# First stage of an attention and feed-forward kernel: the reciprocal's first value in the unit's own PSUM bank, other result latencies for the planner, another order

## The chip, the cores and the metric

The kernel runs on one core of one Trainium2 chip. The metric is the device time of one execution in microseconds (us), the median of several runs. A core has TensorE (PE), which multiplies matrices and writes only PSUM; VectorE (DVE) and ScalarE (ACT), which read and write PSUM and SBUF; GpSimd (POOL), which here works on SBUF only; and SyncE (SP), whose queue issues all DMAs of this kernel. Each engine carries out its instructions in the order of the program. In the profile "PEld" is the loading of a matmul's stationary operand, which overlaps the matmuls.

## The reference

Block-causal attention over 8 batches, 8 heads, 576 positions of width 64 (blocks of 64 positions), and after it a feed-forward layer of 4608 tokens, 512 to 2048 to 512, whose activation is a rational function:

```python
scores = scale * np.matmul(q, k.transpose(0, 1, 3, 2))
scores = np.where(mask, scores, -1000000000.0)      # mask: block_i >= block_j
scores = scores - np.max(scores, axis=-1, keepdims=True)
attn = np.exp(scores)
attn = attn / (np.sum(attn, axis=-1, keepdims=True) + 1e-09)
x = np.matmul(attn, v)                              # then heads side by side: 4608 x 512
h = x @ w_in
h2 = h * h
h3 = h2 * h
P = a[0] + a[1] * h + a[2] * h2 + a[3] * h3
Q = 1.0 + np.abs(b[0]) * np.abs(h) + np.abs(b[1]) * h2
g = P / (Q + 1e-6)
out = g @ w_out
```

All tensors are float32.

## The kernel before

**Precision.** Matmuls run on rounded float32 (fp32r). Each operand is split into a high and a low part, and a product is three matmuls: high by low, high by high, low by high.

**Planner.** Nothing is issued while the kernel is described. Every piece of work becomes an `op` of the class `Plan`: an engine, a planned cost, a priority (`pri`, lower goes first), the buffers it reads and writes, and a function that emits the instructions. `Plan.order` then simulates the engines with the planned costs, takes at each step the operation that can start first (by priority among those that are ready), and the instructions are emitted in that one order, so each engine's queue is fixed by it. `LATENCY` (L66) is the time that the planner adds between the end of an operation and the start of one on another engine that needs it, by the engine that consumes. `PORT` (L65) is added to the planned cost of an operation marked `port=True`, which is used for DVE operations with two operands in SBUF. `gate` holds back an operation until attention has come to within 12 priority units of it.

**Banks.** PSUM's eight banks form one pool, `banks`. A `Buf` takes a slot when its first operation is planned and gives it back after its last. Quotas limit how many banks one use may hold: six for attention (`QA`), two for the first product of a feed-forward unit in the first stage (`QH`), two for its output accumulators (`QO`). The third argument of `Buf` (`keep`) is the number of slots that must stay free when it takes its own.

**Attention.** The eight heads of a batch are taken in pairs, 32 pairs in all, and pair `p` has priorities around `10 * p`. `load` (L380) issues six DMAs for q, k and v; from the third pair on, q and k share one raw buffer. `prep` (L400) transposes q or k on PE (L409) and splits it into high and low on ACT and DVE (L413, L416); for these pairs DMAs copy the parts into the operand tiles `kq`. `vprep` (L441) splits v on ACT and POOL. `scores` (L465) takes five query tiles: score matmuls (L508, L509), maximum on DVE (L520), exponential with sum on ACT (L524), reciprocal of the sum (L531 to L536), normalization on POOL (L538, L544), transposes of the probabilities on PE (L565) and their split on ACT and DVE (L580, L582). `pv` (L589) multiplies with v and writes the result to DRAM scratch (L603 to L621).

**Feed-forward.** The first half of the hidden width is done for 15 chunks of 256 tokens beside attention (`ffn0`, L708, "first stage"), four units per chunk, so 60 units; a unit is 256 hidden values: the first product into one bank `h` (L740), the rational function on 128 x 512 values (`wide`, L675), and the second product (L759). Weights are split by `place` (L625), which `split_weights` (L656) calls: 16 blocks that stay on the chip and 16 that go to DRAM scratch, with priorities spread over a span of attention's. The rest of the feed-forward is done after attention (`ffn1`, L822, "second stage"), whose `wide` calls have `rpsum` set: its reciprocal has a PSUM bank of its own.

**`wide`.** The denominator is built in SBUF tiles: |h| in `ut` (L677), then POOL (L680, L682). The numerator is built in `st` from `h` (L678, L684, L686). The reciprocal of the denominator starts as the exponential of minus its logarithm (L688, L692), is improved by a Newton step (L694, L696) and multiplied with the numerator (L698). ACT and POOL split the result into `gh` and `gl` (L701, L702). In the first stage the reciprocal's first value goes into `vt`, an SBUF tile, so that L694, L696 and L698 have two operands in SBUF.

Of the kernel before, what the change touches and what calls it, by code (L numbers as in the profile page):

```python
# [14 lines left out]
ALU = mybir.AluOpType  # L15
# [13 lines left out]
NFA = 8  # L29
NFB = NF - NFA  # L30
# [4 lines left out]
QC = 1.0 + 1e-6  # L35
# [27 lines left out]


PORT = 220.0  # L65
LATENCY = {"PE": 90.0, "ACT": 40.0, "DVE": 40.0, "POOL": 90.0, "SP": 60.0, "-": 0.0}  # L66


class Plan:
# [161 lines left out]
def attn_ffn_kernel(  # L231
# [22 lines left out]
    banks = Pool([ps.tile([128, 512], F32, name=f"ps{chr(97 + i)}") for i in range(8)])  # L254

    QA, QH, QO, QH1, QO1, QR1, QR = (Pool([None] * n) for n in (6, 2, 2, 2, 4, 2, 1))

    def tiles(pool_, n, shape, dt, name):
# [4 lines left out]
    wscr = ([dpool.tile([128, 4, NFB * 128], F32, name=f"wscri{x}") for x in "hl"]  # L263
            + [dpool.tile([128, NFB, DM], F32, name=f"wscro{x}") for x in "hl"])
# [16 lines left out]
    a0, a1 = coef[:, 0:1], coef[:, 1:2]  # L281
# [9 lines left out]
    QR = tiles(att, 1, [LP, 2 * NL, D], F32, "qr")  # L291
# [88 lines left out]
    def load(p):  # L380
        b, hp = divmod(p, NPAIR)
        h0 = 2 * hp
        pri = 10 * p - 12 + 3
        s = {}
        for which, src in ((0, q), (1, k)):
            r = s["raw", which] = Buf(OS if which and p < NATP else QR)
            for j in range(2):
                aop("SP", sp(147, True), lambda r=r, j=j, src=src: nc.sync.dma_start(
                    out=rows(r)[:, j::2, :], in_=src[b, h0 + j].rearrange("(c p) d -> p c d", p=LP)),
                    wr=[(r, j)], pri=pri + 2 * which)  # L390
        vr = s["vr"] = Buf(VR)
        for j in range(2):
            aop("SP", sp(16, True, 2), lambda j=j: nc.sync.dma_start(
                out=vr.t[j * 64:(j + 1) * 64, 0, :], in_=v[b, h0 + j, 0:64, :]), wr=[(vr, j, 0)], pri=pri + 5)
            aop("SP", sp(131, True), lambda j=j: nc.sync.dma_start(
                out=vr.t[:, 1 + j::2, :], in_=v[b, h0 + j, 64:S, :].rearrange("(c p) d -> p c d", p=128)),
                wr=[(vr, j, 1)], pri=pri + 5)
        return s

    def prep(p, s, which):  # L400
        pri = 10 * p - 10 + (3, 5)[which]
        raw, sc = s["raw", which], (QSCALE, 1.0)[which]
        hl = s["hl", which] = Buf((HLE if p < NATP and p % 2 else HL)[which])
        for half in range(2):
            bank = Buf(banks, QA, 1)

            def tp(half=half, bank=bank):
                for c in range(3):
                    nc.tensor.transpose(bank.t[:, c * LP:(c + 1) * LP], rows(raw)[:, 2 * (half * 3 + c):2 * (half * 3 + c) + 2].rearrange("p j d -> p (j d)"), ident[:LP, :LP])  # L409

            cs = slice(half * 288, half * 288 + 288)
            aop("PE", tr(3, LP), tp, rd=[(raw, 0), (raw, 1), "ident", (hl, "claim")], wr=[bank], pri=pri)
            aop("ACT", act(288), lambda bank=bank, cs=cs: nc.scalar.activation(  # L413
                out=hl.t[:, 0, cs], in_=bank.t[:, :288], func=AF.Copy, scale=sc),
                rd=[bank], wr=[(hl, 0, half)], pri=pri)
            aop("DVE", dve(288), lambda bank=bank, cs=cs: nc.vector.scalar_tensor_tensor(  # L416
                out=hl.t[:, 1, cs], in0=bank.t[:, :288], scalar=sc, in1=hl.t[:, 0, cs].bitcast(F32),
                op0=ALU.mult, op1=ALU.subtract), rd=[bank, (hl, 0, half)], wr=[(hl, 1, half)], pri=pri)
        if p < NATP:
            return  # L420
        H_, L_ = [(hl, 0, 0), (hl, 0, 1)], [(hl, 1, 0), (hl, 1, 1)]
        for j in range(2):
            kq = kqt[p % 2][j]
            own = kq[64 * j:64 * j + 64].bitcast(F32)
            other = kq[64 - 64 * j:128 - 64 * j].bitcast(F32)

            def src(j=j):
                return hl.t[64 * j:64 * j + 64].bitcast(F32)

            def dma(o_, i_, rd, key, kb=147, dims=2):  # L430
                aop("SP", sp(kb * 1.6, dims=3), lambda: nc.sync.dma_start(out=o_, in_=i_()), rd=rd,
                    wr=[("kq", p % 2, j, key)], pri=pri + 0.2 * j)

            if which == 0:
                dma(own[:, 0:2], lambda src=src: src()[:, 0].unsqueeze(1).to_broadcast([64, 2, S]), H_, "q0", 294)
                dma(other[:, 1], lambda src=src: src()[:, 1], L_, "q2")
            else:
                dma(own[:, 2:4], lambda src=src: src(), H_ + L_, "k0", 294)
                dma(other[:, 3], lambda src=src: src()[:, 0], H_, "k1")

    def vprep(p, s):  # L441
        vr = s["vr"]
        pri = 10 * p + 6
        at = [lambda x: x[0:64, 0:64].unsqueeze(1), lambda x: x[64:128, 64:128].unsqueeze(1),
              lambda x: x[:, 128:].rearrange("p (b c) -> p b c", c=192)[:, :, 0:64],
              lambda x: x[:, 128:].rearrange("p (b c) -> p b c", c=192)[:, :, 128:192]]
        of = [lambda: vr.t[0:64, 0:1], lambda: vr.t[64:128, 0:1], lambda: vr.t[:, 1:9:2], lambda: vr.t[:, 2:9:2]]
        keys = [[(vr, 0, 0)], [(vr, 1, 0)], [(vr, 0, 1)], [(vr, 1, 1)]]
        for i, (f, src, rd) in enumerate(zip(at, of, keys)):
            n = 64 if i < 2 else 256  # L450
            vh, vl = (f(x) for x in vpad)
            aop("ACT", (0.833 * n + 110, 0.833 * n + 200), lambda vh=vh, src=src: nc.scalar.copy(out=vh, in_=src()),  # L452
                rd=rd, wr=[("v", i, 0)], pri=pri, after=init_v if p == 0 else ())
            aop("POOL", pool(n, True), lambda vh=vh, vl=vl, src=src: nc.gpsimd.tensor_tensor(  # L454
                out=vl, in0=src(), in1=vh.bitcast(F32), op=ALU.subtract),
                rd=rd + [("v", i, 0)], wr=[("v", i, 1)], pri=pri, after=init_v if p == 0 else ())
# [8 lines left out]
    def scores(p, s, t):  # L465
# [32 lines left out]
        for j in range(2):  # L498
            pri = 10 * p + 2 * t + j
# [47 lines left out]
                    rd=[rc] + [(pt, jj, i) for i in range(np_)], wr=[(pt, "n", jj)], pri=pri)  # L547

        np1 = 128 if t == 0 else nq
        pri += 3  # L550
        nb = 1 + 2 * t
        groups = {1: [1], 3: [1, 2], 5: [1, 4], 7: [4, 3], 9: [3, 3, 3]}[nb]
        blk = 0
        for gi, gn in enumerate(groups):
            bank = Buf(banks, QA, 1)

            def trans(bank=bank, blk=blk, gn=gn):
                for i in range(gn):
# [97 lines left out]
    def split_weights(w, f0, nf, pris, scr):  # L656
        wih, wil, woh, wol = w
        pris = iter(pris)
        for f in range(0, nf, 2):
            cs = slice(f * 128, f * 128 + 256)  # L660
            for d in range(0, 4, 2):
                src = w_in[d * 128:(d + 2) * 128, (f0 + f) * 128:(f0 + f + 2) * 128]
                place(wih[:, d:d + 2, cs], wil[:, d:d + 2, cs], src.rearrange("(d p) f -> p d f", p=128),
                      next(pris), scr, f"wi{f0}_{f}_{d}")
            for d in range(f, f + 2):
                place(woh[:, d:d + 1, :], wol[:, d:d + 1, :],
                      w_out[(f0 + d) * 128:(f0 + d + 1) * 128, :].rearrange("(d p) e -> p d e", p=128),
                      next(pris), scr, f"wo{f0}_{d}")
# [6 lines left out]
    def wide(h, hf, pools, pri, rpsum, xk, tag):  # L675
# [11 lines left out]
            out=st.t, in0=st.t, scalar=a1, in1=h.t, op0=ALU.subtract, op1=ALU.mult), rd=hf, wr=[st], pri=pri)  # L687
        op("ACT", act(512, False, 1), lambda: nc.scalar.activation(out=vt.t, in_=ut.t, func=AF.Ln, bias=qcb),  # L688
           rd=[ut, "qcb"], wr=[vt], pri=pri)
        r0 = Buf(banks, QR1 if rpsum else QR) if rpsum or 0 else vt  # L690
        rq = r0 is vt
        op("ACT", act(512, False), lambda: nc.scalar.activation(out=r0.t, in_=vt.t, func=AF.Exp, scale=-1.0),  # L692
           rd=[] if rq else [vt], wr=[r0], pri=pri)
        op("DVE", dve(512), lambda: nc.vector.scalar_tensor_tensor(  # L694
            out=ut.t, in0=ut.t, scalar=QC, in1=r0.t, op0=ALU.add, op1=ALU.mult), rd=[r0], wr=[ut], pri=pri, port=rq)
        op("DVE", dve(512), lambda: nc.vector.scalar_tensor_tensor(  # L696
            out=r0.t, in0=ut.t, scalar=-2.0, in1=r0.t, op0=ALU.add, op1=ALU.mult), rd=[ut], wr=[r0], pri=pri, port=rq)
        op("DVE", dve(512, 1), lambda: nc.vector.scalar_tensor_tensor(  # L698
            out=st.t, in0=st.t, scalar=a0, in1=r0.t, op0=ALU.subtract, op1=ALU.mult), rd=[r0], wr=[st], pri=pri, port=rq)
        gh, gl = Buf(pools[3]), Buf(pools[4])  # L700
        op("ACT", act(512, False), lambda: nc.scalar.copy(out=gh.t, in_=st.t), rd=[st], wr=[gh], pri=pri)  # L701
        op("POOL", pool(512, True), lambda: nc.gpsimd.tensor_tensor(  # L702
# [81 lines left out]
        pv(p, 0)  # L784
        pv(p, 1)
    op("-", (0, 0), lambda: None, after=early, pri=0, gives=[(X, i) for i in range(3)])
    split_weights(wA, 0, NFA, [0 + 30 * i / NPLA for i in range(NPLA)], False)
    split_weights(wscr, NFA, NFB, [110 + 200 * i / NPLB for i in range(NPLB)], True)
    E0, E1 = 50, 340
    EARLY = ()  # L790
    U0 = [list(range(EARLY[c] if c < len(EARLY) else 4 if c < NCH - 3 else 0)) for c in range(NCH)]
    NU0 = sum(map(len, U0))
# [156 lines left out]
```

## Time and profile before

| | |
|---|---|
| Time, median of 3 runs | 1313.12 us (1309.43 to 1316.41) |
| Profiled execution | 1311.25 us |
| Its span, first to last instruction | 1309.5 us |
| Mean granted clock of TensorE | 0.988 |
| Busy PE / DVE / ACT / POOL | 1245.8 / 972.5 / 893.7 / 898.0 us |
| Busy share PE / DVE / ACT / POOL | 95 / 74 / 68 / 69% |
| Moved by DMA | 195.13 MB, mean 149 GB/s |

A profile is of one execution. In the rows of 40 slices each digit is the busy share of a slice of the span in tenths. Rows of groups end with busy time, mean time of one, idle time of the engine before them and what ended it. Rows of stretches give for each engine the busy time and, in brackets, the number of instructions. Matmuls are pipelined and their ends are modelled, so a PE that reads busy is not always at its peak rate.

### The profile page before, as it was taken

The numbers are of one execution on the slowest core, as the hardware profiler recorded it, in microseconds if no ns is written. First come the engines' busy times: TensorE is split into PE (matmuls) and PEld (weight loads), VectorE is DVE, ScalarE is ACT, GpSimd is POOL, SyncE is SP. The second block draws the span as 40 slices with busy tenths as digits, with TensorE's granted clock in tenths as the row PEclk, the third lists the DMA queues.
The fourth block names the chain that finished last, engine by engine and source line by source line (L and its number), as shares of the span: only waits on it lengthen the run. The fifth ranks groups of instructions, "written<-read, shape, count | busy, mean of one in ns | idle before, by whom it ended". The sixth has DMA issues, their size and how long they took to land.

```text
span 1309.5 us, 23194 instructions
## 1 busy us (share of the span) xinstructions
PE 1245.8 (95%) x7560; PEld 1095.3 (84%) x7560; DVE 972.5 (74%) x1916; ACT 893.7 (68%) x2230; POOL 898.0 (69%) x1218
## 2 busy tenths in 40 slices
PE   7778899999999999999999999999999999999997
PEld 5668799888889888898888889888888888888886
DVE  7877867777778877887887877766666776677665
ACT  5776777777778777787776777655655555555554
POOL 5766876777688867777876777566666666666664
PEclk9888899999999999999999999999999999999999
DMA  5797746777768667768766761750223242324010
GB/s 147 216 240 195 193 126 175 185 181 201 190 169 212 188 178 197 196 190 207 185 181 174 192 179 52 254 189 1 97 88 105 66 129 87 106 66 129 13 53 33
DMA packets 222617, 195.13 MB, mean 149 GB/s; under 512 B 129312, under 2 KB 183584, under 8 KB 222496
## 3 DMA queue, kind: packets, MB, share of 16 engines
q1 hardware_dynamic: 222496, 193.65, 53.8%
q8 instruction: 60, 0.98, 0.3%
q14 instruction: 61, 0.50, 0.1%
HBM read 95.95 MB, written 44.56 MB: 107 GB/s over the span
## 4 chain that ended last, share of the span: by engine, by line
PE 64%; POOL 10%; DMA 8%; DVE 8%; ACT 6%; issue 3%; SPq 1%; POOLq 0%; ACTq 0%; DVEq 0%
PE pse L854 4%; PE psd L854 4%; PE psf L880 4%; PE psg L880 3%; PE psc L880 3%; PE psh L880 2%; PE psb L880 2%; PE psa L880 2%; PE psa L854 2%; PE psb L854 2%; PE psc L759 2%; DMA osa<-in_moe_w_out_dram 2%; PE psh L854 2%; PE psh L740 1%; PE psa L740 1%
## 5 line engine op out<-in xcount | busy, mean ns | idle before, releaser
L680 POOL TENSOR_SCALAR vb<-ua,bab 128x512 f32<-128x512 f32 x58 | 44.8, 772 | 91.1 <-ACT ua L677 90.9
L680 POOL TENSOR_SCALAR va<-ub,bab 128x512 f32<-128x512 f32 x55 | 43.7, 795 | 85.1 <-ACT ub L677 85.0
L454 POOL TENSOR_TENSOR vpl<-vra,vph 128x256 fp32r<-128x256 f32 (+1 forms) x128 | 75.6, 598 | 21.8 <-ACT vph L452 14.5
L702 POOL TENSOR_TENSOR glb<-sa,ghb 128x512 fp32r<-128x512 f32 x60 | 77.7, 1294 | 15.7 <-ACT ghb L701 15.6
L702 POOL TENSOR_TENSOR gla<-sb,gha 128x512 fp32r<-128x512 f32 x57 | 74.1, 1301 | 8.3 <-ACT gha L701 7.7
L682 POOL TENSOR_TENSOR ua<-vb,ua 128x512 f32<-128x512 f32 x58 | 75.9, 1308 | 4.6
L682 POOL TENSOR_TENSOR ub<-va,ub 128x512 f32<-128x512 f32 x55 | 71.3, 1296 | 4.3
L688 ACT ACTIVATE va<-ub,qcb 128x512 f32<-128x512 f32 x55 | 39.8, 724 | 47.9 <-POOL ub L682 47.7
L688 ACT ACTIVATE vb<-ua,qcb 128x512 f32<-128x512 f32 x58 | 42.2, 727 | 41.6 <-POOL ua L682 41.6
L701 ACT CAST ghb<-sa 128x512 fp32r<-128x512 f32 x60 | 37.4, 624 | 22.3 <-DVE sa L698 22.0
L740 PE MATMUL psh<-x,wiha 128*128 128x256 f32 x272 | 51.2, 286 | 0.0
L701 ACT CAST gha<-sb 128x512 fp32r<-128x512 f32 x57 | 35.4, 622 | 10.4 <-DVE sb L698 10.0
L740 PEld LDWEIGHTS psh<-x,wiha 128*128 128x128 f32 x272 | 42.4, 191 | 0.1
L452 ACT CAST vph<-vra 128x256 fp32r<-128x256 f32 (+1 forms) x128 | 39.7, 324 | 2.0 <-POOL vph L322 0.6
L740 PE MATMUL psh<-x,wila 128*128 128x256 f32 x136 | 38.4, 282 | 0.0
L677 ACT ACTIVATE ua<-pse 128x512 f32<-128x512 f32 x25 | 15.0, 600 | 27.2 <-PE pse L854 22.8
L694 DVE SCALAR_TENSOR_TENSOR ub<-ub,pse 128x512 f32<-128x512 f32 x19 | 13.1, 687 | 24.6 <-ACT pse L692 24.6
L694 DVE SCALAR_TENSOR_TENSOR ub<-ub,psd 128x512 f32<-128x512 f32 x18 | 12.4, 688 | 24.7 <-ACT psd L692 24.1
L677 ACT ACTIVATE ua<-psd 128x512 f32<-128x512 f32 x21 | 12.5, 598 | 22.3 <-PE psd L854 20.4
L740 PEld LDWEIGHTS psh<-x,wila 128*128 128x128 f32 x136 | 25.9, 190 | 0.0
L854 PE MATMUL psd<-xxa,wihb 128*128 128x512 f32 x80 | 24.6, 389 | 0.0
L740 PE MATMUL psg<-x,wiha 128*128 128x256 f32 x128 | 24.0, 286 | 0.0
(1666 smaller groups left out, 5673.9 us busy)
## 6 DMA issues: line engine op xcount, KB each, us to landing
xscr<-xsa SPq DMA_DIRECT2D x32, 320.0 KB, 2.4
x<-xscr SPq DMA_DIRECT2D x40, 256.0 KB, 4.1
qra<-in_q_dram SPq DMA_DIRECT2D x64, 144.0 KB, 3.5
qra<-in_k_dram SPq DMA_DIRECT2D x60, 144.0 KB, 2.8
vra<-in_v_dram SPq DMA_DIRECT2D x64, 128.0 KB, 2.6
xscr<-xsa SPq DMA_DIRECT2D x32, 256.0 KB, 3.4
ppa<-pscr SPq DMA_DIRECT2D x15, 512.0 KB, 4.2
osb<-in_moe_w_in_dram SPq DMA_DIRECT2D x10, 512.0 KB, 4.7
```

The source lines that it names most:

```text
L452: aop("ACT", (0.833 * n + 110, 0.833 * n + 200), lambda vh=vh, src=src: nc.scalar.copy(out=vh, in_=src()), rd=rd, wr=[("v", i, 0)], pri=pr ...
L454: aop("POOL", pool(n, True), lambda vh=vh, vl=vl, src=src: nc.gpsimd.tensor_tensor(out=vl, in0=src(), in1=vh.bitcast(F32), op=ALU.subtract ...
L677: op("ACT", act(512), lambda: nc.scalar.activation(out=ut.t, in_=h.t, func=AF.Abs), rd=hf, wr=[ut], pri=pri)
L680: op("POOL", pool(512, False, 2), lambda: nc.gpsimd.tensor_scalar(out=vt.t, in0=ut.t, scalar1=b1, scalar2=b0, op0=ALU.mult, op1=ALU.add), ...
L682: op("POOL", pool(512, True), lambda: nc.gpsimd.tensor_tensor(out=ut.t, in0=vt.t, in1=ut.t, op=ALU.mult), rd=[vt], wr=[ut], pri=pri)
L688: op("ACT", act(512, False, 1), lambda: nc.scalar.activation(out=vt.t, in_=ut.t, func=AF.Ln, bias=qcb), rd=[ut, "qcb"], wr=[vt], pri=pri)
L701: op("ACT", act(512, False), lambda: nc.scalar.copy(out=gh.t, in_=st.t), rd=[st], wr=[gh], pri=pri)
L702: op("POOL", pool(512, True), lambda: nc.gpsimd.tensor_tensor(out=gl.t, in0=st.t, in1=gh.t.bitcast(F32), op=ALU.subtract), rd=[st, gh], wr ...
L740: nc.tensor.matmul(h.t[:, j * CT:(j + 1) * CT], lhsT=w[:, dc, fs], rhs=xb[dc // 2].t[:, dc % 2, hl, :], start=(dc == 0 and i == 0), stop=( ...
L759: nc.tensor.matmul(o[m].t, lhsT=g.t[:, ms], rhs=w[:, f, :], start=(f == 2 * units[0] and i == 0), stop=(f == 2 * units[-1] + 1 and i == 2))
L854: nc.tensor.matmul(h.t, lhsT=w[:, dc, fs], rhs=x.t[:, dc, hl, :], start=(dc == 0 and i == 0), stop=(dc == 3 and i == 2))
L880: nc.tensor.matmul(o[m].t, lhsT=g.t[:, c0:c0 + 128], rhs=w[:, ff, :], start=(a and i == 0 and j == 0), stop=(z and i == 2))
```

## The change

Five things change, all of them in the order or in the first stage:

1. In `wide`, without `rpsum`, the reciprocal's first value goes into `h`'s own bank in place of `vt`. L692 writes `h` and so waits for the last reader of the product (L686); the Newton step and the last product read PSUM; `h` is held until L698. The three DVE operations lose the planned `PORT`.
2. `LATENCY` for consumers on PE goes from 90 to 250 and on POOL from 90 to 150.
3. The priorities of q, k and v loads go down by 3, of q and k preparation by 2, of v's split by 3, of the transposes of the probabilities and their splits by 6.
4. The transposes of the probabilities no longer leave one bank free (`keep` 1 to 0).
5. The 16 weight blocks that stay are spread over 80 priority units in place of 30, the other 16 over 220 in place of 200, and the first stage's units begin at 60 in place of 50.

```diff
-LATENCY = {"PE": 90.0, "ACT": 40.0, "DVE": 40.0, "POOL": 90.0, "SP": 60.0, "-": 0.0}
+LATENCY = {"PE": 250, "ACT": 40,
+           "DVE": 40.0, "POOL": 150, "SP": 60.0, "-": 0.0}
...
-        pri = 10 * p - 12 + 3
+        pri = 10 * p - 12 + 0
...
-        pri = 10 * p - 10 + (3, 5)[which]
+        pri = 10 * p - 10 + (1, 3)[which]
...
-        pri = 10 * p + 6
+        pri = 10 * p + 3
...
-        pri += 3
+        pri += -3
...
-            bank = Buf(banks, QA, 1)
+            bank = Buf(banks, QA, 0)
...
-        r0 = Buf(banks, QR1 if rpsum else QR) if rpsum or 0 else vt
-        rq = r0 is vt
+        r0 = Buf(banks, QR1) if rpsum else h
+        rk = [r0] if rpsum else hf
         op("ACT", act(512, False), lambda: nc.scalar.activation(out=r0.t, in_=vt.t, func=AF.Exp, scale=-1.0),
-           rd=[] if rq else [vt], wr=[r0], pri=pri)
+           rd=[vt], wr=rk, pri=pri)
         op("DVE", dve(512), lambda: nc.vector.scalar_tensor_tensor(
-            out=ut.t, in0=ut.t, scalar=QC, in1=r0.t, op0=ALU.add, op1=ALU.mult), rd=[r0], wr=[ut], pri=pri, port=rq)
+            out=ut.t, in0=ut.t, scalar=QC, in1=r0.t, op0=ALU.add, op1=ALU.mult), rd=rk, wr=[ut], pri=pri)
         op("DVE", dve(512), lambda: nc.vector.scalar_tensor_tensor(
-            out=r0.t, in0=ut.t, scalar=-2.0, in1=r0.t, op0=ALU.add, op1=ALU.mult), rd=[ut], wr=[r0], pri=pri, port=rq)
+            out=r0.t, in0=ut.t, scalar=-2.0, in1=r0.t, op0=ALU.add, op1=ALU.mult), rd=[ut], wr=rk, pri=pri)
         op("DVE", dve(512, 1), lambda: nc.vector.scalar_tensor_tensor(
-            out=st.t, in0=st.t, scalar=a0, in1=r0.t, op0=ALU.subtract, op1=ALU.mult), rd=[r0], wr=[st], pri=pri, port=rq)
+            out=st.t, in0=st.t, scalar=a0, in1=r0.t, op0=ALU.subtract, op1=ALU.mult), rd=rk, wr=[st], pri=pri)
...
-    split_weights(wA, 0, NFA, [0 + 30 * i / NPLA for i in range(NPLA)], False)
-    split_weights(wscr, NFA, NFB, [110 + 200 * i / NPLB for i in range(NPLB)], True)
-    E0, E1 = 50, 340
+    split_weights(wA, 0, NFA, [0 + 80 * i / NPLA for i in range(NPLA)], False)
+    split_weights(wscr, NFA, NFB, [110 + 220 * i / NPLB for i in range(NPLB)], True)
+    E0, E1 = 60, 340
```

## The prediction

> **What bounds the kernel now.** I read the page's slices first, then the first and the last of the first stage's 60 feed-forward units (two of the rows of their opening instruction, L677, where the start times stand last), and then the busy time of each engine in stretches cut at those two times.
>
> ```profile
> PE   7778899999999999999999999999999999999997
> DVE  7877867777778877887887877766666776677665
> PEclk9888899999999999999999999999999999999999
> ```
>
> ```profile
> L677 ACT ACTIVATE ua<-psg x4: 597/598/598, 111.0 to 793.2; 128x512 f32<-128x512 f32 x4
> ...
> L677 ACT ACTIVATE ua<-psf x4: 581/597/600, 316.6 to 839.7; 128x512 f32<-128x512 f32 x4
> ```
>
> ```profile
> 0.00:110.00 110.00, 85.73 (x523) 71.83 (x524) 82.07 (x206) 73.51 (x234) 73.21 (x138) 0.91 0.76 198
> 110.00:150.00 40.00, 35.23 (x252) 31.34 (x250) 33.31 (x69) 29.59 (x85) 32.94 (x44) 1.00 0.85 210
> 150.00:840.00 690.00, 663.18 (x4714) 610.21 (x4715) 539.79 (x1190) 524.66 (x1484) 510.98 (x785) 0.99 0.67 178
> 840.00:1309.00 469.00, 461.68 (x2075) 381.88 (x2073) 317.30 (x452) 265.98 (x429) 280.82 (x253) 1.00 0.28 90
> ```
>
> The columns are PE, PEld, DVE, ACT, POOL, granted clock, DMA share, GB/s. From 840 us PE is busy 461.7 of 469 us: that stage is matmul throughput, its units already keep the reciprocal in PSUM, and nothing in the diff takes a matmul away. I give it zero. What can move lies before 840 us. Up to 110 us PE idles 24.3 us and its clock is 0.91; from 110 to 150 us it idles 4.8; from 150 to 840 us it idles 26.8, while DVE, ACT and POOL are busy 78%, 76% and 74%. No engine but PE is near full, so the idle time of PE comes from its fixed order: a matmul stands at the head of its queue and its input or its bank is late. Visible idle time in all is 55.9 us. It is the nearest row to a ceiling, not a hard one, since a busy PE also hides short gaps between pipelined matmuls.
>
> Whom PE and PEld wait for between 150 and 840 us, for the transposes of the probabilities (L565), the transposes of q and k (L409) and the score matmuls (L508), in that order:
>
> ```profile
>   POOL p2a L544: 10.5, 15
>   POOL p4a L544: 7.1, 14
>   DVE xsa L618: 5.0, 3
>   POOL pkb L538: 3.1, 7
>   POOL p3a L544: 2.5, 5
> ```
>
> ```profile
>   DVE pt2l L582: 6.4, 7
>   DVE xsa L618: 4.0, 2
> ```
>
> ```profile
>   ACT p3a L524: 3.6, 6
>   DVE pt0l L582: 3.6, 6
>   DVE pt2l L582: 2.7, 9
> ```
>
> One stall is partly counted twice here (weight load and matmul). Two kinds stand out: transposes that wait for POOL's normalization (23.2 us), and matmuls that wait for a bank that DVE or ACT still reads (25.3 us).
>
> In the early part the chain of waits from 60 to 150 us reads so:
>
> ```profile
> by line: issue 9.1%; DMA osb<-in_moe_w_out_dram 7.7%; DMA osa<-in_moe_w_in_dram 7.5%; DMA kqbb<-hl1a 7.0%; DMA kqab<-hl1a 5.9%; DMA osa<-in_moe_w_out_dram 5.5%; DMA x<-xscr 4.2%; PE psb L603 3.9%; DVE pt2l L582 2.3%; DMA qra<-in_q_dram 2.3%
> ```
>
> ```profile
> 60.00:80.00 20.00, 14.09 (x87) 12.38 (x86) 14.33 (x37) 14.12 (x46) 11.81 (x24) 0.83 0.96 243
> 80.00:100.00 20.00, 13.70 (x88) 10.70 (x87) 16.59 (x44) 16.07 (x53) 15.44 (x29) 0.98 0.93 249
> ```
>
> Three weight loads make 20.7% of these 90 us, 18.6 us, and the DMA engines are 96% and 93% busy. Here the end is set by DMA, and by DVE and ACT queues that stand behind a weight that has not landed.
>
> **The change, part by part.**
>
> *The reciprocal in the unit's own bank.* The lines L694, L696, L698 (DVE) and L692 (ACT), each before and after 840 us; in the first row of a pair the value lies in SBUF, in the second in PSUM. The second number is the busy time, with the count behind it:
>
> ```profile
> 0.00:840.00 840.00, 50.52 (x60) 0.98 0.69 182
> 840.00:1309.00 469.00, 57.79 (x84) 1.00 0.28 90
> ...
> 0.00:840.00 840.00, 48.18 (x60) 0.98 0.69 182
> 840.00:1309.00 469.00, 58.98 (x85) 1.00 0.28 90
> ...
> 0.00:840.00 840.00, 49.98 (x59) 0.98 0.69 182
> 840.00:1309.00 469.00, 63.92 (x85) 1.00 0.28 90
> ...
> 0.00:840.00 840.00, 38.20 (x60) 0.98 0.69 182
> 840.00:1309.00 469.00, 50.58 (x84) 1.00 0.28 90
> ```
>
> Per instruction: 842 against 688 ns, 803 against 694, 847 against 752, and 637 against 602 for ACT. DVE loses 154 + 109 + 95 = 358 ns a unit, 21.5 us over 60 units; ACT loses 35 ns, 2.1 us. How much reaches the end? At least nothing: DVE has 22% idle and every saving can end as longer idle. At most 21.5 us. PE's waits for DVE in the rows above are 21.7 us; half of that, for the double count, is 11 us, and DVE's load between 150 and 840 us falls by 20.4 of 539.8 us, under 4%, so only a part goes. I take **-4 us**, nearer to the row of waits than to the row of DVE time.
>
> POOL's share of this: L682, the product of two SBUF tiles that runs beside those DVE instructions.
>
> ```profile
> 0.00:840.00 840.00, 78.82 (x60) 0.98 0.69 182
> 840.00:1309.00 469.00, 109.11 (x84) 1.00 0.28 90
> ```
>
> It takes 1314 ns before and 1299 after 840 us: 15 ns, 0.9 us in all. The cost of two SBUF operands falls on DVE, hardly on POOL, and I give POOL zero. The Trainium skill (SBUF — State Buffer, Who interferes with whom) states that a DVE instruction with two SBUF inputs and a GpSimd instruction that reads SBUF lock each other out, and that whoever starts first blocks the other fully. The trace agrees on DVE's side (842 against 688 ns) and shows little of the other; by a symmetric rule POOL would gain up to another 21 us of busy time and the sum would be larger by a part of that, which no row here supports.
>
> *The bank is held longer, and Exp gains a wait.* One unit whole: the first rows are PE's and ACT's, then DVE's.
>
> ```profile
> 612.41 0.40 PE L740 MATMUL psh<-x,wiha 128*128 128x256 f32 x2
> ...
> 618.94 0.75 DVE L686 SCALAR_TENSOR_TENSOR sa<-sa,coef,psh 128x512 f32<-128x512 f32 x1
> ...
> 623.81 0.63 ACT L692 ACTIVATE vb<-vb 128x512 f32<-128x512 f32 x1
> ...
> 628.05 0.74 DVE L698 SCALAR_TENSOR_TENSOR sa<-sa,coef,vb 128x512 f32<-128x512 f32 x1
> ```
>
> Before, the bank is free after L686: 7.3 us. Now it is held to the end of L698: 16.4 us. Sixty units in 729 us (111 to 840) are one per 12.3 us (59 steps), so by this unit the h banks in use rise from 0.6 to 1.3 of the two allowed, and six banks, less these, are what attention has beside the two accumulators: 5.4 become 4.7. L692 now waits for L686, which here was done 4.1 us earlier, so the wait is covered. Where it isn't, ACT's exponentials (L524) and copies (L580) stand behind it, and transposes wait for them. Unknown price: from 0 to the 25.3 us of bank waits once more. The diff also lets a probability transpose take the last free bank (the reserve of one becomes zero), which works the other way. I take **+3 us**, an eighth of the row of bank waits: attention loses 0.7 of 5.4 banks, 13%, and I let its bank waits grow in that share.
>
> *Result latencies, earlier transposes.* The planner now counts 250 instead of 90 before a PE consumer, 150 instead of 90 before a POOL one, so it puts other matmuls ahead of a transpose whose input comes late. The 41 waits for POOL before L565 quoted above hold 23.2 us; if each shrank by the 160 + 60 ns that the plan now adds, that is 9 us, 4.5 after the double count. The transposes' priority moves by 6 units to the front, with their copies on ACT and DVE, which pushes back the score matmuls, the first products and whatever waits behind them. From +5 (as much lost as could be won) to -9, I take **-5 us**.
>
> *Weights over a longer time, loads and preparation earlier, first units later.* The first 16 weight blocks get priorities 0 to 75 instead of 0 to 28, and the reserve of DMA work per attention pair goes down early, where 18.6 us of the chain are weight loads. A third of it is 6 us. The six loads per pair go ahead by 3 units, past scratch writes and key copies on SP's queue, and the two preparations by 2; v's split by 3 on ACT and POOL. SP's instructions are in order, so a load that waits for the one raw buffer holds those behind it. That limits the gain. The first units start a pair later (60 for 50, ten units a pair). Five pairs' worth of units had passed when the first unit came at 111 us, so a pair takes 22 us early; PE idles 24.3 of 110 us there and its clock is 0.91, so a late start costs up to 22 x 0.22 + 22 x 0.09 = 7 us if the pairs don't get faster. Between -12 and +7 I take **-6 us**, nearer to the chain's row, because most of the weights were landing late anyhow. The Trainium skill (TensorE: Matmul & The Clock Gate, What's actually happening) says that an idle window of about 3.4 us puts the clock to half. The clock's row of 0.91 in the idle stretch bears it out in direction, and it speaks against a later start.
>
> **Sum:** -4 + 3 - 5 - 6 = -12 us. The profiled execution took 1311.25 us (span 1309.5 and 1.75 around it), 1.87 below the median of the runs shown. So it would go to 1299.3, and the median from 1313.1 to **1301 us**.
>
> **Rivals.**
>
> *Bank shortage.* The two units' banks are both held when units follow within 16.4 us, which is the mean case at 12.3. Then scores and transposes queue for banks. For it: 25.3 us of such waits already. Against it: DVE's own share shrinks and the reserve is dropped. Decided from where a third of the units overlap through their whole hold. Price: waits double, +25, less the 15 of the sum's other terms, +10: 1323 us.
>
> *Waits swap places.* DVE isn't the bound, the planner's order only moves the late operand from POOL to ACT, and the late start eats the early gain of DMA. -4 at DVE, +3 for banks, and 0 for the rest: 1312 us. For it speaks that three engines sit at 74 to 78% alike.
>
> *All of it lands.* Half of DVE's 21.5 (-11), all of the latency term (-9), two thirds of the weight loads (-12) and banks free: 1281 us. For it: the ceiling of 55.9 us has room.
>
> **How the numbers follow.** About 0.5% (6.6 us) is what a measurement of this kernel can tell from no change. The forecast, 1291 to 1306, gets 0.47; all lands 0.13; waits swap 0.26; bank shortage 0.14. Faster 0.60, same 0.26, slower 0.14. Both signs don't hold the chance evenly, and a range from 1284 to 1319 leaves out about one tenth on each side: most of the case in which all lands, and bank shortage at its full price.
>
> **What would show it.** DVE's L694, L696 and L698 at 690 to 750 ns before 840 us, with the reciprocal written to an h bank, show the first step; POOL's L682 near 1300 the second. If banks are short, waits of L508, L409 and L740 for L698 or L582 grow. If latencies help, the waits of L565 for L544 fall below 20 us. If the early part helps, PE idles less than 24 us before 110 us and the weight loads leave the chain. The prediction is wrong if the last unit ends no earlier than 835 us, or if PE begins to idle in the second stage.

## The result and the profile after

The changed kernel takes 1278.9 us (1278.76 to 1279.91, 4 runs) against 1312.32 us before: a ratio of 0.9745, 95% interval 0.9718 to 0.9772. It is 33.4 us faster, where 12 were forecast, and 5 us below the range. The profiled execution took 1278.76 us, its span 1276.6. Lines of the first stage's code stand one lower than before, so L566 here is L565 there.

The slices of the page, and the stretches (PE, PEld, DVE, ACT, POOL, clock, DMA share, GB/s), cut at the last unit, which now opens at 801.3 us:

```profile
PE   7879999999999999999999999999999999999997
DVE  7867887778787777778876876666676777677664
PEclk8989999999999999999999999999999999999999
```

```profile
0.00:110.00 110.00, 86.66 (x568) 73.14 (x569) 79.84 (x209) 75.86 (x247) 72.08 (x139) 0.89 0.79 205
110.00:150.00 40.00, 37.36 (x255) 31.89 (x253) 37.91 (x89) 34.29 (x105) 32.05 (x54) 1.00 0.80 202
150.00:800.00 650.00, 637.78 (x4632) 595.34 (x4632) 503.66 (x1162) 511.43 (x1446) 459.56 (x771) 1.00 0.70 184
800.00:1276.00 476.00, 468.79 (x2111) 388.04 (x2110) 320.88 (x458) 269.85 (x434) 284.82 (x256) 1.00 0.29 94
```

The same middle stretch before:

```profile
150.00:800.00 650.00, 623.30 (x4444) 573.47 (x4445) 511.05 (x1143) 499.00 (x1428) 483.92 (x754) 0.99 0.68 181
```

The second stage did not move: PE idles 7.2 us after the last unit, before 7.3. The 33 us came out of the first stage, whose last unit opens at 801 instead of 840 us; some 5 of these 38 us go back, because more matmuls are then still to do (2111 against 2075 behind the cut). PE's visible idle time fell from 29.0 to 26.0 us before 150 us and from 26.7 to 12.2 us between 150 and 800 us. That is 17.5 us; the rest is not idle time in this view but a denser stream, 4632 matmuls in the same 650 us instead of 4444. Over the whole execution PE's busy time fell from 1245.8 to 1230.6 us for the same 7560 matmuls. The mean granted clock, 0.988 before and 0.990 after, gives by estimate some 3 us of that, not more. In the middle stretch ACT and DVE did more instructions too, and POOL did 17 instructions more in 24 us less.

Who kept PE and PEld waiting from 150 to 800 us, for the probabilities' transposes (L566), the score matmuls (L509) and the transposes of q and k (L410):

```profile
  POOL pkb L539: 5.3, 11
  POOL p2a L545: 4.3, 8
  POOL p3a L545: 3.5, 8
```

```profile
  DVE pt2l L583: 4.4, 9
  ACT vb L689: 0.9, 2
```

```profile
  ACT sb L679: 1.3, 1
  DMA qra<-in_k_dram: 1.1, 1
```

Both kinds of wait shrank. All the listed rows in which the probabilities' transposes wait for POOL hold 15.3 us between these times, 26.1 before. The rows of L509 and L410 that name DVE or ACT hold 8.3 us, 23.8 before, and the waits of L410 for banks that DVE still reads, 10.4 us before, are gone.

The three DVE lines (L695, L697, L699), first stage above second stage:

```profile
0.00:801.00 801.00, 40.34 (x59) 0.99 0.72 188
801.00:1276.00 475.00, 58.42 (x85) 1.00 0.29 93
...
0.00:801.00 801.00, 40.23 (x59) 0.99 0.72 188
801.00:1276.00 475.00, 59.58 (x86) 1.00 0.29 93
...
0.00:801.00 801.00, 42.94 (x58) 0.99 0.72 188
801.00:1276.00 475.00, 64.28 (x86) 1.00 0.29 93
```

They take 684, 682 and 740 ns in the first stage, nearly as in the second (687, 693 and 747). This is what the first step foretold.

POOL is where the reading before the result went wrong. Its normalization (L544), the product for the packed keys (L538) and the split of v (L454), 150 to 800 us, before:

```profile
150.00:800.00 650.00, 124.08 (x202) 0.99 0.68 181
...
150.00:800.00 650.00, 68.97 (x127) 0.99 0.68 181
...
150.00:800.00 650.00, 58.82 (x100) 0.99 0.68 181
```

and after:

```profile
150.00:800.00 650.00, 111.19 (x205) 1.00 0.70 184
...
150.00:800.00 650.00, 54.42 (x127) 1.00 0.70 184
...
150.00:800.00 650.00, 52.38 (x100) 1.00 0.70 184
```

614 became 542 ns, 543 became 429, 588 became 524. With the counts of after that is 14.8 + 14.5 + 6.4 = 36 us of POOL's time, more than DVE's own saving. Over the whole execution POOL is busy 848.5 us instead of 898.0 with the same 1218 instructions, DVE 942.3 instead of 972.5.

The timelines of the two engines before the change show where that time was lost. The first product below runs alone, the second beside L694 and L696:

```profile
169.17 0.40 POOL L538 TENSOR_TENSOR pka<-p3a,rcc 128x128 f32<-128x128 f32 x1
...
174.64 0.67 DVE L694 SCALAR_TENSOR_TENSOR ua<-ua,vb 128x512 f32<-128x512 f32 x1
174.86 0.70 POOL L538 TENSOR_TENSOR pkb<-p4a,rce 128x128 f32<-128x128 f32 x1 [1.71 <-DVE rce L536]
175.34 0.77 DVE L696 SCALAR_TENSOR_TENSOR vb<-ua,vb 128x512 f32<-128x512 f32 x1
```

From 150 to 800 us, 41 of the 127 products L538 overlap one of the three DVE lines; these take 714 ns on average, the other 86 take 464. L682, the line read before the result, overlaps them in only 7 of 52 cases, and takes 1401 ns there and 1297 otherwise. DVE shows the same: L694, L696 and L698 take 847, 836 and 843 ns where they overlap an instruction of POOL, and 683, 684 and 740 in the 25 cases where they don't, no more than with the operand in PSUM. After the change overlap costs nothing: 422 against 431 ns for the product, 686 against 685 for L695. So what two SBUF operands cost here is the contention between the two engines.

### The profile page after: what moved, and what is told of

It is laid out like the page before. It is cut to its first block, busy times and chain, and to the rows that moved or that the text cites. A ratio compares the mean times of both kernels' runs of the same rounds, so it can differ in the third digit from the quotient of the medians.

```text
span 1276.6 us, 23262 instructions
## 1 busy us (share of the span) xinstructions
PE 1230.6 (96%) x7560; PEld 1088.4 (85%) x7560; DVE 942.3 (74%) x1916; ACT 891.4 (70%) x2230; POOL 848.5 (66%) x1218
## 4 chain that ended last, share of the span: by engine, by line
PE 68%; DVE 7%; DMA 7%; ACT 7%; POOL 6%; issue 3%; SPq 1%; POOLq 0%; ACTq 0%; DVEq 0%
PE psd L855 4%; PE psf L855 4%; PE psb L881 4%; PE psh L881 4%; PE pse L881 3%; PE psg L881 3%; PE psf L604 3%; DMA osa<-in_moe_w_in_dram 3%; PE psc L881 2%; PE psa L881 2%; PE psa L855 2%; PE psc L855 2%; PE psc L760 2%; PE psg L855 1%; PE psa L741 1%
## 5 line engine op out<-in xcount | busy, mean ns | idle before, releaser
L703 POOL TENSOR_TENSOR glb<-sa,ghb 128x512 fp32r<-128x512 f32 x58 | 75.5, 1302 | 20.1 <-ACT ghb L702 17.7
L683 POOL TENSOR_TENSOR ub<-va,ub 128x512 f32<-128x512 f32 x60 | 77.9, 1299 | 4.6
L455 POOL TENSOR_TENSOR vpl<-vra,vph 128x256 fp32r<-128x256 f32 (+1 forms) x128 | 67.8, 539 | 19.5 <-ACT vph L453 11.6
L702 ACT CAST ghb<-sa 128x512 fp32r<-128x512 f32 x58 | 36.1, 622 | 26.8 <-DVE sa L699 26.7
L702 ACT CAST gha<-sb 128x512 fp32r<-128x512 f32 x58 | 36.2, 624 | 11.1 <-DVE sb L699 10.9
L695 DVE SCALAR_TENSOR_TENSOR ub<-ub,psf 128x512 f32<-128x512 f32 x23 | 15.8, 686 | 25.5 <-ACT psf L693 25.4
L695 DVE SCALAR_TENSOR_TENSOR ub<-ub,psd 128x512 f32<-128x512 f32 x21 | 14.4, 687 | 26.5 <-ACT psd L693 26.3
L741 PE MATMUL psa<-x,wiha 128*128 128x256 f32 x176 | 33.2, 288 | 0.5 <-DVE sb L699 0.4
L741 PE MATMUL psf<-x,wiha 128*128 128x256 f32 x176 | 32.8, 285 | 0.5 <-DMA x<-xscr 0.5
L678 ACT ACTIVATE ua<-psf 128x512 f32<-128x512 f32 x25 | 15.0, 598 | 25.3 <-PE psf L855 21.1
L703 POOL TENSOR_TENSOR glb<-sb,ghb 128x512 fp32r<-128x512 f32 x14 | 18.1, 1296 | 16.1 <-ACT ghb L702 16.1
L741 PEld LDWEIGHTS psa<-x,wiha 128*128 128x128 f32 x176 | 27.3, 191 | 1.1 <-DVE sb L699 0.6
L741 PEld LDWEIGHTS psf<-x,wiha 128*128 128x128 f32 x176 | 27.5, 191 | 0.7 <-DMA x<-xscr 0.7
L741 PE MATMUL psb<-x,wiha 128*128 128x256 f32 x144 | 27.0, 286 | 0.0
```

The costliest lines, as they stand in the source:

```text
L695: op("DVE", dve(512), lambda: nc.vector.scalar_tensor_tensor(out=ut.t, in0=ut.t, scalar=QC, in1=r0.t, op0=ALU.add, op1=ALU.mult), rd=rk, w ...
L741: nc.tensor.matmul(h.t[:, j * CT:(j + 1) * CT], lhsT=w[:, dc, fs], rhs=xb[dc // 2].t[:, dc % 2, hl, :], start=(dc == 0 and i == 0), stop=( ...
```

## The experiments

All medians are set against the runs of the kernel before that were taken beside them (1312.3 to 1314.6 us); the changed kernel is 1278.9.

### One part alone, and all but one

Four parts: the reciprocal (with the planned port cost of its three DVE operations), the latencies, the priorities of attention's pieces (with the kept bank), and the weights' spread with the units' start. Each kernel takes the lines of one part, or of all the others, from the diff shown above.

```diff
# alone: kernel before with this part of the diff; all but: changed kernel with this part undone
reciprocal:  r0 = Buf(banks, QR1) if rpsum else h ... (no port=rq)
latencies:   LATENCY = {"PE": 250, ..., "POOL": 150, ...}
priorities:  load +0, prep (1, 3), vprep +3, transposes -3, Buf(banks, QA, 0)
weights:     80 * i / NPLA, 220 * i / NPLB, E0 = 60
```

> Kernel before with only the reciprocal's first value in h's bank (its planned port cost goes with it); all latencies, priorities and spreads as before. Theory L (the planner's latencies carry most of the gain): -4 us or less, 1306 to 1312. Theory D (DVE's 21.5 us carries it): -15 us or more, below 1298. Theory O (each order is a throw of its own and the parts don't add): anywhere from -12 to +12, and it and its counterpart (all but this) don't add up to -33.

> Changed kernel with the reciprocal's first value back in SBUF and its planned port cost back. Theory L: near the changed kernel, 1280 to 1288. Theory D: 1293 or more. Theory O: anything between 1275 and 1300.

> Kernel before with only the planner's latencies 250 (PE) and 150 (POOL). Theory L: -15 us or more, below 1298, with PE's waits for POOL before L565 down from 23 us to under 15. Theory D: within 5 us of before. Theory O: -12 to +12.

> Changed kernel with the planner's latencies back at 90. Theory L: 1294 or more. Theory D: 1280 to 1286. Theory O: anything between 1275 and 1300.

> Kernel before with only the earlier loads, preparations, v splits and transposes, and no bank kept back for transposes. Theory L: within 6 us of before. Theory Q (the order of attention's pieces carries the gain, not the latencies): -12 us or more. Theory O: -12 to +12.

> Changed kernel with the priorities of loads, preparations, v splits and transposes and the kept bank as before. Theory L: 1280 to 1286. Theory Q: 1291 or more. Theory O: anything between 1275 and 1300.

> Kernel before with only the weight blocks spread wider and the first stage's units from 60 on. My prediction had -6 us for this part, with PE's idle time before 110 us falling below 24 us. Theory L: -6, 1306. Theory O: -12 to +12.

> Changed kernel with the weight blocks' spread and the units' start as before. By the prediction's term 1285. Theory O: anything between 1275 and 1300.

| part | alone, us | ratio to before (95%) | all but it, us | worse than the changed kernel by |
|---|---|---|---|---|
| reciprocal | 1322.12 | 1.0072 (1.0045 to 1.0099) | 1314.59 | 35.7 |
| latencies | 1313.35 | 1.0002 (0.9985 to 1.0019) | 1295.21 | 16.3 |
| priorities | 1320.62 | 1.0051 (1.0032 to 1.0069) | 1299.41 | 20.5 |
| weights | 1330.67 | 1.0110 (1.0066 to 1.0154) | 1311.10 | 32.2 |

No part alone makes the kernel faster. Alone they cost 9.0, 0.2, 6.9 and 16.9 us, together they bring 33.4, and undoing one costs 16 to 36. Theory L, theory D and theory Q fall: undoing the part that each of them names costs what it said, but no part brings the gain alone. Theory O's ranges hold for five of the eight kernels; the weights alone (16.9, beyond 12) and all but the reciprocal and all but the weights (above 1300) lie outside. Two signs were written down besides. With the latencies alone the transposes still wait 22.1 us for POOL, not under 15. With the weights alone PE idles 23.3 us before 110 us, below 24 as forecast, but 35.7 instead of 26.7 us between 150 and 800. Two questions follow: what does the reciprocal's place give on the chip, and what makes it worthless alone?

The second has an answer in the trace of the kernel with the reciprocal alone. Its waits of the first product (L740), of the score matmuls (L508) and of the transposes of q and k (L409):

```profile
  DVE sb L698: 7.9, 9
  ACT p2a L524: 1.9, 2
```

```profile
  DVE pt2l L582: 6.7, 12
  DVE pt1l L582: 6.2, 6
  ACT ub L677: 4.7, 2
```

```profile
  DVE ua L694: 5.3, 2
```

The first product now waits for the last reader of an earlier unit's bank (L698), which no matmul waited for before, and the score matmuls wait for banks still read by a unit or by attention's splits. All rows that name DVE hold 8.8 us for L740 (0.7 before) and 13.8 for L508 (6.6 before); those of L409 did not grow (8.2, 10.4 before). In the same trace the transposes of the probabilities wait only 12.7 us for POOL instead of 26.1. So what POOL gives back comes out again as waits for banks. This is the bank shortage of the rivals.

### The same order with two SBUF operands again

This separates the chip from the planner: the instructions of every engine stay in the same order, and only where the second operand lies changes. The rational function's values in the first stage are not the reference's.

```diff
-        rk = [r0] if rpsum else hf
+        rk, rt = ([r0], lambda: r0.t) if rpsum else (hf, lambda: wA[2][:, 0, :].bitcast(F32))
...
-            out=ut.t, in0=ut.t, scalar=QC, in1=r0.t, ...
+            out=ut.t, in0=ut.t, scalar=QC, in1=rt(), ...      # likewise in the two after it
```

> Changed kernel, every instruction in the same order on every engine, but L695, L697 and L699 of the first stage read a resident weight tile in SBUF in place of the reciprocal in PSUM, so they have two SBUF operands again (the feed-forward's numbers in the first stage aren't the reference's). It asks what the chip itself gives back for the operand's place, apart from any new order. Theory H (the place frees DVE and, through it, POOL's small attention instructions; the order only makes use of it): 15 us or more above the changed kernel, 1294 to 1312, and POOL's normalization (L545) back from some 735 to 810 ns for 512 columns. Theory R (the new order carries the gain): within 6 us of the changed kernel, under 1285.

> The same edit on the kernel that has only the reciprocal moved (1322 us), order unchanged on every engine (the feed-forward's numbers in the first stage aren't the reference's). Theory H: slower than 1322 by 10 us or more, since there the freed time was already spent on the longer bank hold: 1332 or above. Theory R: within 6 us of 1322.

The first took 1293.67 us (0.9865 of before, 0.984 to 0.9891): 14.8 us above the changed kernel. The second took 1333.64 us, 11.5 above the kernel with the reciprocal alone. The thresholds written down beforehand were 15, just missed, and 10, so theory H holds for a part: 11 to 15 us come from the operand's place in both of the orders tried. The second figure is the less sure, since its four runs spread from 1330.7 to 1342.4 us. In the first kernel DVE's three lines take 770, 822 and 865 ns between 150 and 800 us. POOL's same three lines from 150 to 800 us in the first of them:

```profile
150.00:800.00 650.00, 135.70 (x206) 1.00 0.71 183
...
150.00:800.00 650.00, 64.10 (x127) 1.00 0.71 183
...
150.00:800.00 650.00, 59.65 (x102) 1.00 0.71 183
```

They are back at 659, 505 and 585 ns, with nothing changed on POOL itself. And PE's waits before the transposes of the probabilities grew where they had shrunk:

```profile
  POOL p3a L545: 8.3, 16
  POOL p2a L545: 6.7, 16
  POOL pkb L539: 5.8, 13
```

8.3 + 6.7 + 5.8 is 20.8 us against 13.1 in the changed kernel's three rows; all rows for POOL hold 28.0 against 15.3. The Trainium skill (SBUF — State Buffer, Who interferes with whom) says that a DVE instruction with two SBUF inputs and a GpSimd instruction that reads SBUF exclude each other; these runs agree on both sides, 61 to 116 ns on the means of POOL's three lines (against the changed kernel) included. The edit differs from the old code in two ways: L697 still writes PSUM, and L695 no longer reads what ACT's L693 wrote. DVE's waits for L693, 15.7 us before L695 in the changed kernel between 150 and 800 us, are 0.8 us before L697 here, so if anything the edit understates the cost. It moves both engines at once; POOL's share and DVE's share of the 11 to 15 us are not parted.

The other 18.6 us (1312.31 less 1293.67) belong to the rest of the change, with the contention in place: the new order and the bank's longer hold. Theory R holds for that part.

### Does an order move the time by chance?

```diff
-           "DVE": 40.0, ...
+           "DVE": 42.0, ...        # in the changed kernel, and in that with the reciprocal alone
-LATENCY = {..., "ACT": 40.0, ...
+LATENCY = {..., "ACT": 41.0, ...   # in the kernel before
```

> Changed kernel with the planner's latency for DVE at 42 in place of 40: means nothing, but about half of the instructions come in another order. Theory O (each order is a throw): 8 us or more away from the changed kernel, most likely slower, 1287 to 1305. Theories H and R: within 6 us of it.

> The kernel that has only the reciprocal moved, with the planner's latency for DVE at 42. Theory O: 8 us or more away from 1322, as likely faster. Theories H and R: within 6 us of it.

> Kernel before with the planner's latency for ACT at 41 in place of 40, which puts most of PE's instructions in another order and means nothing. The two nudges so far moved 5.5 and 3.2 us, both up. Theory O: 8 us or more from before. Otherwise within 6 us of it.

They took 1284.43, 1325.35 and 1317.15 us: 5.5, 3.2 and 2.6 us above their own kernels, with about a fifth of PE's order new in the second and most of it in the other two. Three draws are few, but none reached 8 us. Such a nudge moves these kernels by some 5 us, and differences below that are not read here. It does not bound what a larger change of order can do: e14 below has the changed kernel's instructions and is 29.9 us slower.

### What the longer hold and the planned cost are worth

```diff
# e13, changed kernel: the SBUF tile of the logarithm is held until the last product
-            ... op0=ALU.subtract, op1=ALU.mult), rd=rk, wr=[st], pri=pri)
+            ... op0=ALU.subtract, op1=ALU.mult), rd=rk + [vt], wr=[st], pri=pri)
# e14, changed kernel: the three DVE operations carry the planned port cost again
+            ..., port=not rpsum)
# e15, kernel before: the unit's bank is held until the last product
-            ... rd=[r0], wr=[st], pri=pri, port=rq)
+            ... rd=[r0] + ([] if rpsum else hf), wr=[st], pri=pri, port=rq)
# e17, all but the reciprocal: without the planned port cost
-            ..., port=rq)
+            ...)
# e18: kernel before with the reciprocal and the weights' part of the diff
```

> Changed kernel, but the SBUF tile of L689 and L693 is held until the last product, as it was before the change (there it carried the reciprocal). Theory V (the tile that comes free five us sooner lets units and weight blocks follow each other, and this is the rest of the gain): 1288 or more. Theory P (the planner's true DVE cost is the rest) and theory B (the new priorities clear the bank waits): within 6 us of 1279.

> Changed kernel, but the planner still adds its 220 for the shared port to the three DVE operations of the first stage; the instructions are the same, only their order changes. Theory P: 1288 or more. Theories V and B: within 6 us of 1279.

> Kernel before, reciprocal in SBUF as it was, but the unit's bank is held until the last product. It prices the longer hold by itself. If the hold is what ate the chip's gain in the kernel that has only the reciprocal moved: 12 us or more slower than before, 1324 to 1340, with more waits of L508, L409 and L740 for DVE. If it isn't: within 6 us of 1313.

> Changed kernel with the reciprocal back in SBUF (1314.6 us so far), but without the planner's 220 for the port on the three DVE operations: the chip's contention stays, only the plan's cost goes. Theory P (the plan's smaller DVE cost is by itself worth what the contention at fixed order leaves over, some 18 us): 1290 to 1300. Theory T (the plan's cost has to be true to the chip; a cost that is too small is as bad as one that is too large): 1308 or more.

> Kernel before with the reciprocal moved (1322 alone) and the weight blocks' spread and units' start (1331 alone). If the weights' spread is what repairs the longer bank hold, as its 32 us in the changed kernel suggest: 1300 or less. If it works only together with latencies and priorities: 1310 or more.

**The tile** (e13): 1278.84 us. Its earlier release is worth nothing; PE's order did not even change. Theory V falls.

**The hold** (e15): 1331.90 us, 1.0130 of before (1.0097 to 1.0164). Holding the bank longer, with the reciprocal left in SBUF, costs 17.3 us. The prediction had taken 3. The time lies in the range written down, but the sign that went with it is missing: no matmul waits for L698, and the rows of L508, L409 and L740 that name DVE hold 12.4 us, less than the 17.7 before. The planner knows of the longer hold and makes another order, and the cost came through that order; how, this trace does not show. As a sum it fits the reciprocal alone: 17.3 lost, 11.5 won on the chip at its order, 5.8 lost together, against 9.0 measured, a difference no larger than a nudge makes.

**The planned cost** (e14): 1308.83 us, 29.9 above the changed kernel, with the same instructions. Theory P's bound is met, but a third of it is one event. PE's longest wait between 108 and 152 us there:

```profile
PE psf L566 <- DVE sb L699: 11.3, 1, 11.3
```

In the chain of waits of that stretch DVE stands behind a weight that lands late, the unit's last product behind it, and a transpose for the bank:

```profile
130.12 5.84 DMA osb<-in_moe_w_out_dram
135.97 2.04 DVE sa L637
138.04 1.64 DVE sa L640
...
144.74 0.67 DVE sb L699
```

So here a unit that held a bank tied PE to what stopped DVE. PE idles 13.7 us between 110 and 150 us, 2.6 in the changed kernel. Some 19 us are left for the rest of the stage.

**The planned cost with the contention kept** (e17): 1319.32 us, 4.7 above the same kernel with the port in the plan, no gain at all. Theory P falls here and theory T fits: the smaller planned cost paid where the chip keeps it (e14), not by itself.

**The weights with the reciprocal** (e18): 1308.81 us, 0.997 of before (0.9951 to 0.999). Spreading the weights costs 16.9 us without the reciprocal and brings 13.3 with it (from 1322.12). The time lies between the two ranges written down, near the one by which the weights' spread works only with the rest. It repairs a part of what the hold costs, less than the 22 us that would have made it the whole cure. With latencies and priorities besides, another 29.9 us come. Latencies and priorities without the weights are 1311.10, 11.0 below the reciprocal alone. So each half repairs 11 to 13 us and both together 43.2.

**What stays open.** Why the repairs add up to more than their sum is not shown. In the changed kernel the waits for banks are short, and in the reciprocal alone and in e14 some are long, which fits a picture in which PE's fixed order stops at whatever is left late, but no run here proves that picture. Why the new order keeps 18.6 us of its gain with the contention put back (1293.67), while all but the reciprocal keeps none (1314.59, and 1319.32 without the port in the plan), is not settled either: the one that is faster holds the bank longer, though the hold by itself was dear.

## Why the prediction was wrong, step by step

- **Where the time goes.** Right: second stage 0 us, everything from the first, no engine but PE near full.
- **DVE's durations.** Right to 12 ns: 842, 803 and 847 became 684, 682 and 740, where 688, 694 and 752 were read.
- **"The cost of two SBUF operands falls on DVE, hardly on POOL, and I give POOL zero."** This is the step that failed. It was read from L682 as an instruction that runs beside those of DVE. It comes before L694 in the unit's own chain and overlapped the three lines in 7 of 52 cases. POOL's other instructions do run beside them: L544, L538 and L454 gave back 36 us from 150 to 800 us. The symmetric rule of the Trainium skill (SBUF — State Buffer, Who interferes with whom), set aside there, was the better guide. The term for the operand's place was -4 us and measured -11 to -15.
- **The bank's longer hold, +3 us.** Mis-sized: 17.3 us alone, and not through the waits for banks from which the 3 us were scaled: with the hold alone the rows of L508, L409 and L740 that name DVE or ACT hold 23.7 us, 24.5 before. In the changed kernel it is covered: the rows of L509 and L410 that name DVE or ACT hold 8.3 us, 23.8 before.
- **Latencies and earlier transposes, -5 us.** Alone, latencies measure +0.2 and priorities +6.9; in the changed kernel they are worth 16.3 and 20.5. The waits that they were to shorten, those of the transposes for POOL, fell from 26.1 to 15.3 us between 150 and 800 us. The runs lay that chiefly to the operand's place: the reciprocal alone brings them to 12.7, the weights alone to 16.8 and the latencies alone to 22.1, the priorities alone raise them to 36.9, and the changed kernel with two SBUF operands has 28.0.
- **Weights and early part, -6 us.** Wrong in kind. PE's idle time before 110 us went from 24.3 to 23.3 us, so the early stretch gave 1 us, and 2.1 more up to 150 us; the clock there was 0.89, not better than 0.91. Yet the part is worth 32.2 us in the changed kernel, and most of its effect lies later: without it PE idles 5 us more before 150 us and 9.3 more between 150 and 800 (31.0 against 26.0, 21.5 against 12.2).
- **The sum.** The deeper fault: four terms were added as if each were worth the same with and without the others. Measured alone the four parts add up to +33.0 us, and together they make -33.4. At the changed kernel's own order the miss of 21.4 us falls into two halves: the operand's place, -4 forecast and -14.8 measured, and the rest, +3 - 5 - 6 = -8 forecast and -18.6 measured. Why the rest is worth 18.6 stays open. The case "all of it lands" came within 2 us of the time (1281), but by other amounts than those it was made of.
- **The rivals.** Bank shortage was real in the reciprocal alone, and so was a swap of waits, from POOL to DVE: PE's weight loads there wait 10.4 us for POOL (22.1 before) and 21.8 for DVE (14.5 before), from 150 to 800 us. In the changed kernel neither came.

## What to carry to other kernels

When an operand moves from SBUF to PSUM, count what it frees on the engines that worked beside it (here POOL, 36 us), over all of their instructions that overlap it, and count the bank's longer hold at the same time; here the two were 11 to 15 and 17 us and hid each other. Where a planner fixes the order, try a structural change together with a new choice of its parameters before dropping it: the same edit was 9 us slower with the old ones and part of 33 us faster with the new ones. Test parts at a fixed order as well as alone, since only that separates the chip from the plan.

## What was not expected of the hardware

Two SBUF operands cost DVE nothing measurable by themselves here: L694 took 683 ns where no POOL instruction overlapped it and 847 where one did, and 684 with the operand in PSUM. On POOL the cost went to whatever overlapped: the products for the packed keys (L538) went from 543 to 429 ns once DVE's second operand lay in PSUM, while the 1300 ns ones (L682, L702), which seldom overlapped, stayed within 1.3%. ACT wrote the exponential a little faster into PSUM as well: in the first stage from 150 to 800 us, 635 ns before and 605 after.
